# A mixed attention and Fourier kernel on one core: mirrored sequence rows regrouped by period, copied back by one DMA per batch, with a new instruction order

## The chip, the core and the metric

The kernel runs on one NeuronCore of one Trainium2 chip. The time is the device time of one execution, in microseconds (us). The core has five engines with an instruction queue of their own each: TensorE (PE, matrix products and transposes), VectorE (DVE), ScalarE (ACT), GpSimd (POOL) and SyncE (SP). In this kernel SP does nothing but issue DMAs, one after the other, and nearly every DMA of the kernel goes through it. Sixteen DMA engines move the bytes.

## What is computed

```python
# attention, for each batch and head:  q, k, v: (8, 8, 576, 64), omega: (128, 64)
def phi(x):                              # x is q or k times 64**-0.25
    h = einsum('bhsd,md->bhsm', x, omega) - sum(x * x, -1, keepdims=True) / 2
    return exp(h - max(h, -1, keepdims=True)) / sqrt(128)
kv  = einsum('bhsm,bhsd->bhmd', phi(k), v);  z = sum(phi(k), axis=2)
att = einsum('bhsm,bhmd->bhsd', phi(q), kv) / (einsum('bhsm,bhm->bhs', phi(q), z) + 1e-6)
x   = att, heads side by side            # (8, 576, 512)
# Fourier mixing and a two-layer block
u   = x + real(fft(fft(x, axis=1), axis=2))
un  = (u - mean(u)) / sqrt(var(u) + 1e-6)          # over the last axis
out = u + relu(un @ w_ch1) @ w_ch2                 # 512 -> 2048 -> 512
```

## The kernel before

**Two stages.** The first stage (0 to 446 us of the profile) does the attention and the Fourier mixing of all 8 batches, converts the weights, which arrive as 64-bit numbers, to 32 bits (`narrow`), prepares sums of weight blocks for the second stage (`w2_parts`), and already runs the two-layer block for the first four tiles of 128 rows (`plain`, L1017 and L1040). The second stage (446 us to the end) runs the two-layer block for the other 4,096 rows in 8 blocks of 512, with products arranged as in Strassen's scheme (L1224 and L1403).

**Attention.** A unit of work is a pair of heads; there are 4 per batch, 32 in all, and three streams of them run side by side. One pair loads k and q (L376, L379) and v (L384), transposes them on PE (L505, moved out of PSUM by ACT in L516), multiplies with omega (L587), takes maxima on DVE (L531) and exponentials on ACT (L548), forms the sums over the keys (L621), transposes phi(q) (L505 again, moved out by ACT in L522), multiplies (L669, L677) and divides (L686 to L698). A partition of the loaded tiles holds 9 consecutive rows of the sequence (R = 9).

**Rows and slots.** The result of a batch is kept in a tile x of 128 partitions and 5 slots of 512 numbers. The rows stand in an order that suits a real Fourier transform over the sequence: slot 0 holds rows t, slot 3 rows 288 + t, slots 1 and 2 the mirrored rows 288 - t and 576 - t, and slot 4 what is left. Before the change, the rows t of a slot are grouped by the half of an 18-row period that they lie in (`half`, 64 partitions each), then by remainder (`QUAD`), then by period (16). This order is made in `evicted` (L522): a 128x256 eviction writes 16 consecutive numbers at a time, and the third group is read backwards as a whole (`back`).

**Mixing.** `mix` folds x, multiplies with tables of cosines and sines (`_tables`, L781 to L840), and `residual` adds the result to x slot by slot (L879, L880, on POOL or DVE) and stores the sums to a DRAM buffer `us` in natural row order. Slots 0, 3 and 4 go there directly, each in two DMAs (L894). For slots 0 and 3 the destination of such a DMA is four remainders by 16 periods, the remainders outermost. Slots 1 and 2 hold mirrored rows, whose order has to be reversed; each is stored to a second DRAM buffer `uh` by one DMA (L886), and when all five slots have landed, 8 DMAs (L911) copy `uh` to `us`, two for each of four remainders, reading the periods backwards. Each moves 64 KB, written as 4 outer pieces by 32 rows of 128 numbers.

**Who reads it.** `norm_of` loads a tile of 128 rows of `us` (L920 into u), takes the statistics on DVE (L947 to L949), a power on POOL (L951), scales on DVE (L953) and transposes on PE (L957). In the first stage 8 such tiles are made: four for `plain`, four for the first block of the second stage. The four final sums of `plain` load the same rows again (L920 into ur).

**What sets the order.** Each engine runs a fixed list of instructions. The lists are written by `Listing.run`: every stream of work yields steps with an engine, a planned duration and planned events, and the string `PICKS` says for each turn which waiting stream goes next. The planned durations and events decide only the order; the real waits are semaphores that follow from which instruction reads what another one wrote. So an instruction that is listed too early holds up all that stands behind it on its engine, and a DMA on SP whose data isn't ready holds up all later DMAs. The second stage is listed without `PICKS`, by the planner's own rule.

Of the kernel before, what the change touches and what calls it, by code (L numbers as in the profile page):

```python
# [17 lines left out]
F32 = mybir.dt.float32  # L18
# [10 lines left out]
QUAD = (2, 4, 6, 8)  # L29
MIRROR = (7, 5, 3, 1)  # L30
ORDER_R = (0,) + QUAD + MIRROR
# [8 lines left out]
class Clock(NamedTuple):  # L40
# [23 lines left out]
    "130dc0debe3dedefedeef3aae8bfg0cijbkfa98j88i8i8if2gfQehgjeeeekfjk7fklhggdgeidhiQfed7gfgbga8898jiiaigf"  # L64
    "ig9IHaaebbibbgilhhfhfgbjkhhhliOJKTfe9ich888i88jh9hg8aijkfhPg8hhdhhfdidfdfg8799ggI8i8jaghgl88ekkfejff"
    "fdjhdjgfjdegghk1IccjejeiidLcibkihek798kjml6jMgec9c9Gg6iiiShefjjJg7jejj66bgkakddkejmeediigihfbhfifhde"
    "fjifkkbaOkkcllmfi8ijNakeeemkhcM7oo7ckk6obM9nmfj9bad97hfmf8lfmmd8nnkHUdeeediicS7ifedbfifgcfefggeegcai"
    "dgejciegdgcgfciehffQihffhhdhdhhda79li07hi64678j9jii577gdjji5gdghachcfcgdOif5gcFgfbfbcfge5i6697k7l37a"
    "9gidbehdjc6hhkd7lc8jbejkl9bhihjja6cfi76jcjcbf8lmfnDciidbhg5icVfghkoba9aagadgfekbdbh9KG9k7ggdlie7cjai"
    "bmgegigfalkijfIcegdjeTejdgfQehd88i864NcbfagH8g7ghkdfdd6hfeijbgbff67eahacf6g8g7be54N6e9ccdafbdecccb5d"  # L70
    "hccd957hh5he86l878gg77ldWddifdfhejgg6gRi6Gdafjb8aQdkdj5cgddfigfdafhdQficdhefe9hhhfL55f5hai6b696inlhh"
    "h6MecljcnijVlcdcchhhcf96afdijiif5bjQhfhgghHIeiabjiijg87jjcf6d5iijiiMaajha87mWekfkjUjgjbeifddg5gihf5N"
    "4ehbceh4bfibcgabcckefcfdjjfhedcklfiighed4ifkfdlemcbdd655kjme9dmb5hiVkckkal79jjlEdmijhkhnnklod5hhgmfF"
    "mcmdeedllkeedjId787hLF8ahahhg68fkgjifggkh5iedhijkeddeglhf7ckk3ejbkmk7ck8f7ik6jj5j5744mn76nnjjeiaakj5"
    "4mfgogjiU5Ofll6ecjgfflTkjg5Ob8hceflafi5675lk869llan9VV3775ll86kf7khjaQi6gkklic5lhk5nnndfgikk59aiicja"
    "ifjbfhihaebdmngffbI61efcgdh0cgf89EO6ii9hceOcbafdfda8d27995fc5bPa779dgdeIR9QSa8Md9cg9d99eb3bag79JMbbc"
    "ceddbe9PKbbaacccc32d9de8e5379dfKb9f2ded6adbc79cd8ceca8e9dceHaHeebbaaeabc98K5977b8aee8hifdbcdfccad9d3"
    "added6Ocae85d233babb9c9c8c463c83K97a777cbdc687daIb9df9cabgae9769egeHb993ee89P5e8biafiihbec6jk8hkkFgj"
    "153ki32fdgL3a484f5e4bcb4b97bL62eeFefcffKI2d7d794abIJ4134a79917GK3ab46b9962738a7cc79cc33aLMJI64effbcc"
    "b4ebdfObec2ccLceacec68aOa8ee625G69c9M6bddcJd7a98aa27bbLb5dc6eag5b6f5fee98bd91dfddBfgQdfQI5477523c881"  # L80
    "a0b3444Ebb9a089aKa88aba8a177bcdeHLOa13ad76cc4Fd8c7cca80a64966667d547840965bc8bbe65507dcb1d732D697174"
    "6968G5624408A7E66A35555555011001110"
# [167 lines left out]
def _tables(S, DM):  # L250

    half, rr, ph = (a.ravel() for a in np.meshgrid(np.arange(2), QUAD, np.arange(16), indexing="ij"))
    t = 9 * (2 * ph + half) + rr
    t0 = 9 * (2 * np.arange(32)[None, :] + np.arange(2)[:, None])
    ks = [np.concatenate([t[64 * g : 64 * g + 64], S // 2 - t[64 * g : 64 * g + 64], t0[g]]) for g in range(2)]
    turns = [(t[:, None] * k) % S for k in ks]
    turns.append((np.tile(t0.ravel(), 2)[:, None] * np.concatenate(ks)) % S)
    turn = np.concatenate(turns, axis=1)  # L260
    ang = 2.0 * np.pi * turn / S
    cs = np.cos(ang)
    sn = np.where(turn * 2 % S == 0, 0.0, np.sin(ang))

    d = np.arange(DM // 4)[:, None]
    k = np.arange(DM // 2 + 1)
    k = np.concatenate([k[k % 4 == 0], k[k % 4 == 2], k[k % 2 == 1]])[None, :]  # L270
    turn = (d * k) % DM
    cd = np.cos(2.0 * np.pi * turn / DM)
    turn = (np.where((d == 0) & (k % 2 == 1), DM // 4, d) * k) % DM
    sd = np.where(turn * 2 % DM == 0, 0.0, np.sin(2.0 * np.pi * turn / DM))
    return {
        n: np.ascontiguousarray(a).astype(np.float32)
        for n, a in dict(cs=cs, sn=sn, cd=cd, sd=sd).items()
    }
# [3 lines left out]
def kernel(  # L282
# [86 lines left out]
    def loads():  # L369
        for n in range(B * NP):  # L370
            b, pr = divmod(n, NP)
            h = slice(2 * pr, 2 * pr + 2)
            rows = "i (p r) d -> (i p) r d"
            yield Step(SP, 0.45, 3.0, take=("kq",), kb=288)
            kq = ld.tile([P, 2 * R, D], F32, name="kq", tag="kq")
            nc.sync.dma_start(kq[:, 0:R, :], k[b, h].rearrange(rows, r=R))  # L376
            kqs[n] = kq
            yield Step(SP, 0.45, 3.6, makes=("kq", n), kb=288, bias=-2.98)
            nc.sync.dma_start(kq[:, R : 2 * R, :], q[b, h].rearrange(rows, r=R))  # L379

    def load_v(n):
        b, pr = divmod(n, NP)
        yield Step(SP, 0.6, 4.0, take=(f"vd{n % NV}",), makes=("vd", n), kb=500, bias=0.52)
        nc.sync.dma_start(  # L384
            vds[n % NV][:, :, 0:D],
            v[b, 2 * pr : 2 * pr + 2].rearrange("i (p r) d -> (i p) r d", r=R),
        )
# [27 lines left out]
    def load_tables():  # L415
        yield Step(NONE, after=(("kq", 2),))
        for n, a in tabs.items():
            yield Step(SP, 1.0, 4.0, makes=n, kb=a.nbytes / 1024, bias=0.92)
            src = nc.inline_tensor(a, name="k_" + n).ap()
            for p0, p1 in ((0, 96), (96, a.shape[0])):  # L420
                nc.sync.dma_start(tab_sb[n][p0:p1], src[p0:p1])
# [35 lines left out]
    def weights():  # L457
# [4 lines left out]
        for i, (dst, src) in enumerate(parts):  # L462
# [3 lines left out]
            else:  # L466
                yield Step(SP, 0.5, 4.2, take=("slab",), makes=("raw", i), kb=512)
# [9 lines left out]
    uh = [dram.tile([8, 2, 16, DM], F32, name=f"uh{b}") for b in range(B)]  # L477
# [10 lines left out]
    def transposed(src, name, groups, after, makes, give, back=None, order=None):  # L488
# [3 lines left out]
        for j0, j1 in groups:  # L492
# [13 lines left out]
            yield Fork(evicted(dst, b, j0, j1, makes, (j0, j1) == back, order))  # L506
        return dst

    def evicted(dst, b, j0, j1, makes, back, order):
# [3 lines left out]
        ps = ps[:, :, ::-1] if back else ps  # L513
# [5 lines left out]
        dst = dst.rearrange("q c p -> q (c p)").rearrange("q (h s c t) -> q s c h t", h=h, s=s, t=t)  # L519
        ps = ps.rearrange("q c (h t s) -> q s c h t", h=h, s=s)  # L520
        for i in range(s):
            nc.scalar.activation(out=dst[:, i], in_=ps[:, i], func=AF.Copy)  # L522
# [32 lines left out]
    def attn(n):  # L555
# [74 lines left out]
        def keep():  # L630
# [19 lines left out]
            (5, R),  # L650
# [13 lines left out]
        for i in range(2):  # L664
            for c in range(4):
                j0, back = (5, 1) if c in (1, 2) else (1, 0)
                c0 = 128 * (j0 + 2 * (i ^ back) + c % 2)
                for g in range(2):
                    nc.tensor.matmul(  # L669
                        ndp[D * g : D * g + D, i, (D + 1) * c : (D + 1) * (c + 1)],  # L670
                        lhsT=flat[:, c0 + D * g : c0 + D * g + D],
                        rhs=kvs[0][:, i, :],
                    )
# [36 lines left out]
    def mix(b):  # L710
# [102 lines left out]
        for c in range(NC3):  # L813
# [39 lines left out]
            yield Fork(residual(b, c, x, abb))  # L853

    def residual(b, c, x, abb):
# [18 lines left out]
        def summed(g, left, right):  # L874
# [9 lines left out]
            yield Step(SP, 0.42 if slot in (1, 2) else 0.84, 2.6, makes=("us", b, slot), kb=2 * np_, bias=-0.92)  # L884
            if slot in (1, 2):
                nc.sync.dma_start(uh[b][:, 2 - slot], u)  # L886
                return
            for s in range(2):
                rows = rows_of(b, s)
                if slot == 4:  # L890
                    rows = rows[0]
                else:
                    rows = rows[2::2, 16 * (slot == 3) : 16 * (slot == 3) + 16]
# [5 lines left out]
        yield Step(NONE, after=(("us", b, c if c < NL else 4),), give=("bmp",), bias=1.09)  # L899
        if c == NL:  # L900
            yield Step(
                SP, 3.4, 4.0,
                after=tuple(("us", b, i) for i in range(5)),
                makes=("us", b),
                give=(f"x{b % 2}",),
                kb=512,
            )
            for s in range(2):
                for n, r in enumerate(MIRROR):
                    back = uh[b][4 * (1 - s) + n].rearrange("e t (i d) -> (e t) i d", i=4)  # L910
                    nc.sync.dma_start(  # L911
                        rows_of(b, s)[r].rearrange("p (i d) -> i p d", i=4),
                        back[::-1].rearrange("p i d -> i p d"),
                    )

    def rows_of(b, s):
        return us[S * b : S * (b + 1), :].rearrange("(p s r) d -> s r p d", s=2, r=R)[s]
# [20 lines left out]
    def norm_of(j, t, i, pool, dst):  # L938

        yield Step(SP, 0.5, 3.0, take=("u",), kb=256)  # L940
# [107 lines left out]
    def rest(t, b, yp):  # L1048
        yield Step(SP, 0.5, 2.7, take=("ur",), kb=256)
# [41 lines left out]
    def w2_parts():  # L1091
# [22 lines left out]
        for i, made_of in (  # L1114
# [16 lines left out]
            yield Step(SP, 2.2, 4.5, after=(("w2t", i),), kb=7 * 256, makes=("w2l", i))  # L1131
# [409 lines left out]
```

## Time and profile before

| what | value |
|---|---|
| median of 3 runs | 1207.48 us (1206.46 to 1210.01) |
| the profiled execution: its own time, its span in the profile | 1205.58 us, 1203.7 us |
| granted TensorE clock, mean | 0.993 |
| PE busy in the first stage (446 us) and the second (757.7 us) | 419.2 us, 752.3 us |
| DVE busy in the two stages | 321.6 us, 381.7 us |
| ACT busy in the two stages | 297.2 us, 170.1 us |
| POOL busy in the two stages | 180.3 us, 238.7 us |
| DMAs L911 (uh to us): count, median SP time of one issue | 64, 628 ns |
| DMAs L894 (x to us): the same | 48, 538 ns |
| DMAs L886 (x to uh): the same | 16, 599 ns |

The profile is of one execution, so durations read from it are summed against its own 1205.58 us; the 1.9 us between that and the span lie around the profiled instructions. The median of the runs is 1.9 us above the profiled execution. A row of the table of stretches gives the stretch in us from the start and its length, then the busy time of each engine with the number of instructions begun, then the granted PE clock as a share of full speed, the mean busy share of the 16 DMA engines, and GB/s. A row of a timeline gives start, length, engine, line, operation, tiles written and read, the number of merged instructions, and in square brackets how long the engine had been idle before and what it waited for. "L911" is line 911 of the kernel.

### The profile page before, as it was taken

Reading aid. Unit: us, or ns where it says so; the run is one execution under the profiler, and the core shown is the slowest. Engines: PE = TensorE matmul, PEld = TensorE weight load, DVE = VectorE, ACT = ScalarE, POOL = GpSimd, SP = SyncE. Lnnn points to the kernel's source line nnn. Section 1 sums busy time; section 2 is a strip of 40 time slices with the busy share of each in tenths; the row PEclk is TensorE's granted clock in tenths of the full one; section 3 lists DMA queues with packets and bytes.
Section 4 is the critical chain, followed back from the end, with each engine's and each line's share of the span. In section 5 each row is a group of like instructions: output and inputs, shape, how many; then the busy total and the mean of one; then the engine's idle time right before and its main releaser. Section 6 shows DMA issues by size and latency. Waiting matters only on the chain.

```text
span 1203.7 us, 31915 instructions
## 1 busy us (share of the span) xinstructions
PE 1171.5 (97%) x12753; PEld 1049.2 (87%) x12753; DVE 703.3 (58%) x1496; ACT 467.3 (39%) x1585; POOL 419.0 (35%) x490
## 2 busy tenths in 40 slices
PE   7898999999999999999999999999999999999998
PEld 6777888779959778998998999999899899899898
DVE  4896998977664553572472474374275276267245
ACT  6887888767646112222222222222222222222211
POOL 2453443542433324314323323422421431430421
PEclk9998999999989999999999999999999999999999
DMA  9655756657553343482383294195086176167145
GB/s 261 184 144 161 219 178 193 187 156 228 187 166 111 115 133 117 161 283 91 122 293 120 82 295 158 43 303 190 9 297 194 44 257 207 62 224 249 62 162 189
DMA packets 148452, 205.71 MB, mean 171 GB/s; under 512 B 48720, under 2 KB 62288, under 8 KB 148304
## 3 DMA queue, kind: packets, MB, share of 16 engines
q1 hardware_dynamic: 147936, 203.54, 53.6%
q8 instruction: 101, 1.65, 0.6%
q14 instruction: 47, 0.39, 0.1%
q10 hardware_dynamic: 368, 0.13, 0.0%
HBM read 171.90 MB, written 35.91 MB: 173 GB/s over the span
## 4 chain that ended last, share of the span: by engine, by line
PE 78%; DMA 1%; DVE 1%; SPq 1%; ACT 0%; issue 0%; DVEq 0%; ACTq 0%
PE banks L1224 32%; PE banks L1403 29%; PE banks L1017 4%; PE banks L1040 3%; PE banks L505 2%; PE banks L587 2%; PE banks L957 1%; PE banks L669 1%; PE banks L621 1%; PE banks L829 1%; PE banks L781 1%; DMA u<-us 1%; DMA kq<-in_q_dram 1%; PE banks L791 1%; PE banks L840 0%; ACT e L548 0%
## 5 line engine op out<-in xcount | busy, mean ns | idle before, releaser
L1210 DVE CUSTOM_DVE_ANT_0 hid<-banks,s 128x256 f32<-128x256 f32 x192 | 79.7, 423 | 255.3 <-PE banks L1224 250.4
L1403 PE MATMUL banks<-wl,sums 128*128 128x128 f32 x1792 | 217.5, 275 | 0.0
L1403 PEld LDWEIGHTS banks<-wl,sums 128*128 128x128 f32 x1792 | 208.9, 192 | 0.5
L1238 ACT ACTIVATE s<-banks 128x256 f32<-128x256 f32 x192 | 73.7, 384 | 260.6 <-PE banks L1224 245.8
L548 ACT ACTIVATE e<-banks,nmx 128x128 f32<-128x128 f32 x576 | 163.2, 422 | 29.1 <-DVE nmx L531 26.2
L1224 PE MATMUL banks<-unT,w 128*128 128x256 f32 x704 | 167.5, 379 | 0.0
L1224 PEld LDWEIGHTS banks<-unT,w 128*128 128x128 f32 x704 | 132.7, 190 | 17.9 <-issue 0.5
L1378 ACT ACTIVATE s<-banks 128x128 f32<-128x128 f32 x168 | 46.6, 278 | 242.5 <-PE banks L1403 195.9
L1224 PE MATMUL banks<-tt,w1s 128*128 128x256 f32 x512 | 126.2, 379 | 0.0
L1291 POOL TENSOR_TENSOR hs<-hid 128x256 f32<-128x256 f32 x64 | 46.5, 726 | 205.0 <-DVE hid L1210 178.6
L1224 PEld LDWEIGHTS banks<-tt,w1s 128*128 128x128 f32 x512 | 97.2, 190 | 13.3
L531 DVE TENSOR_REDUCE nmx<-banks 128x8 f32<-128x1024 f32 (+1 forms) x96 | 89.4, 951 | 23.0 <-PE banks L587 21.7
L1383 DVE TENSOR_TENSOR part<-banks,s 128x128 f32<-128x128 f32 x168 | 48.9, 291 | 89.2 <-PE banks L1403 89.0
L1403 PE MATMUL banks<-wl,hid 128*128 128x128 f32 x768 | 97.6, 275 | 0.0
L1403 PEld LDWEIGHTS banks<-wl,hid 128*128 128x128 f32 x768 | 93.5, 192 | 1.2
L1291 POOL TENSOR_TENSOR hs<-hid,hs 128x256 f32<-128x256 f32 x64 | 46.5, 728 | 120.1 <-issue 95.2
L587 PE MATMUL banks<-om,kqT 64*64 64x128 f32 x2304 | 79.4, 277 | 2.0 <-issue 0.7
L1224 PE MATMUL banks<-unT,w1s 128*128 128x256 f32 x320 | 80.6, 379 | 0.0
L587 PEld LDWEIGHTS banks<-om,kqT 64*64 64x64 f32 x2304 | 64.3, 134 | 14.0 <-issue 6.0
L951 POOL TENSOR_TENSOR rstd<-rstd,mhalf 128x1 f32<-128x1 f32 x36 | 24.5, 682 | 146.4 <-DVE rstd L949 146.4
L1403 PE MATMUL banks<-wl,hs 128*128 128x128 f32 x576 | 74.9, 275 | 0.4 <-DVE part L1383 0.4
L1403 PEld LDWEIGHTS banks<-wl,hs 128*128 128x128 f32 x576 | 70.0, 192 | 0.9 <-DVE part L1383 0.6
(126 smaller groups left out, 1958.1 us busy)
## 6 DMA issues: line engine op xcount, KB each, us to landing
wl<-w2l SPq DMA_DIRECT2D x392, 256.0 KB
raw<-in_moe_w_ch_dram SPq DMA_DIRECT2D x32, 512.0 KB
kq<-in_k_dram SPq DMA_DIRECT2D x32, 288.0 KB
kq<-in_q_dram SPq DMA_DIRECT2D x32, 288.0 KB
vd<-in_v_dram SPq DMA_DIRECT2D x32, 288.0 KB
u<-us SPq DMA_DIRECT2D x36, 256.0 KB
ur<-us SPq DMA_DIRECT2D x36, 256.0 KB
out_dram<-ur SPq DMA_DIRECT2D x34, 256.0 KB
```

The source lines that it names most:

```text
L531: nc.vector.tensor_reduce(nmx[:, :, 0:num], pps[:, :, 0 : MF * num].rearrange("p b (c m) -> p b c m", m=MF), axis=AX.X, op=ALU.max, negate ...
L548: nc.scalar.activation(out=e[:, c + (i if num == 1 else 0), :], in_=pps[:, i, MF * c : MF * c + MF], func=AF.Exp, bias=nmx[:, i, c : c + 1],)
L587: nc.tensor.matmul(pps[cols, c, MF * m : MF * m + MF], lhsT=kqT[rows, j, cols], rhs=om2[rows, :],)
L1017: nc.tensor.matmul(hp[:, 0:TP], lhsT=w1[:, dc, 128 * fc : 128 * fc + 128], rhs=unTs[key][:, dc, :], start=(dc == 0), stop=(dc == NDC - 1),)
L1040: nc.tensor.matmul(yp[:, 0:DM], lhsT=hs[fc][:, 128 * i : 128 * i + 128], rhs=w2[:, fc, :], start=(fc == 0), stop=(fc == NFC - 1),)
L1210: nc.vector._custom_dve(TENSOR_ADD_SAT, out=o, in0=ps, in1=sb, s0=FMAX, s1=0.0)
L1224: nc.tensor.matmul(ps[:, 0:HT], lhsT=left(dc), rhs=right(dc), start=start and dc == 0, stop=(dc == D2 - 1), skip_group_check=True,)
L1238: nc.scalar.activation(out=s[:], in_=ps[:, 0:HT], func=AF.Copy)
L1291: nc.gpsimd.tensor_tensor(out=o, in0=l, in1=r, op=op)
L1378: nc.scalar.activation(out=s[:], in_=ps[:, 0:128], func=AF.Copy)
L1383: nc.vector.tensor_tensor(out=part[:, t, 128 * m : 128 * m + 128], in0=ps[:, 0:128], in1=saved[with_][:], op=ALU.add,)
L1403: nc.tensor.matmul(ps[:, 0:128], lhsT=left[:, f], rhs=wls[j, i, n][:, f], start=start and f == 0, stop=(f == 3), skip_group_check=True,)
```

## The change

The rows of a slot are now grouped by even and odd remainder (`EVEN` and `ODD`, 64 partitions each), then by period, then by remainder. Four consequences follow in the code:

- In `evicted` the number of ACT instructions stays, but the 128x256 ones now write with the four remainders innermost, so that consecutive numbers in reading order land 4 numbers (16 bytes) apart, and the second of each two reads both the remainders and the periods backwards.
- `mirrored` takes the place of the two L886 stores. It stands behind both sums and sends slots 1 and 2 together in two DMAs of 256 KB.
- One DMA of 512 KB takes the place of the 8 DMAs L911. It copies 8 consecutive rows for each of 32 periods, the periods read backwards, in 16 outer pieces by 32 rows of 256 numbers.
- The stores of slots 0 and 3 (two DMAs each, as before) now have 16 periods outermost and four remainders inside.

The planned durations of several DMAs are changed, and `PICKS` is a new string (1,851 picks; before, 1,835). The tables keep their shapes. In the core of the diff, `PICKS`, the changed offsets of the L669 products and seven changed planned durations are left out:

```diff
-QUAD = (2, 4, 6, 8)
-MIRROR = (7, 5, 3, 1)
-ORDER_R = (0,) + QUAD + MIRROR
+EVEN = (8, 6, 4, 2)
+ODD = (7, 5, 3, 1)
+ORDER_R = (0,) + EVEN + ODD
...
-    half, rr, ph = (a.ravel() for a in np.meshgrid(np.arange(2), QUAD, np.arange(16), indexing="ij"))
-    t = 9 * (2 * ph + half) + rr
+    t = np.array([18 * ph + r for rows in (EVEN, ODD) for ph in range(16) for r in rows])
...
-    uh = [dram.tile([8, 2, 16, DM], F32, name=f"uh{b}") for b in range(B)]
+    uh = [dram.tile([32, 8, DM], F32, name=f"uh{b}") for b in range(B)]
...
-        ps = ps[:, :, ::-1] if back else ps
...
-        dst = dst.rearrange("q c p -> q (c p)").rearrange("q (h s c t) -> q s c h t", h=h, s=s, t=t)
+        dst = dst.rearrange("q c p -> q (c p)").rearrange("q (h s t c) -> q s c h t", h=h, s=s, t=t)
         ps = ps.rearrange("q c (h t s) -> q s c h t", h=h, s=s)
         for i in range(s):
-            nc.scalar.activation(out=dst[:, i], in_=ps[:, i], func=AF.Copy)
+            of = ps[:, i, ::-1, :, ::-1] if i and j0 else ps[:, i]
+            nc.scalar.activation(out=dst[:, i], in_=of, func=AF.Copy)
...
+        yield Fork(mirrored(b, x))
+
+    def mirrored(b, x):
+        yield Step(SP, 1.15, 2.6, after=(("sum", b, 1), ("sum", b, 2)), makes=("uh", b), kb=512, bias=-0.92)
+        for s in range(2):
+            nc.sync.dma_start(
+                uh[b].rearrange("(e t) (n s) d -> s (t n) e d", e=2, s=2)[s],
+                x[64 * s : 64 * s + 64, 2:0:-1, :],
+            )
...
             if slot in (1, 2):
-                nc.sync.dma_start(uh[b][:, 2 - slot], u)
+                yield Step(NONE, makes=("sum", b, slot))
                 return
+            yield Step(SP, 1.15, 2.6, makes=("us", b, slot), kb=2 * np_, bias=-0.92)
+            p0 = 16 * (slot == 3)
             for s in range(2):
-                rows = rows_of(b, s)
                 if slot == 4:
-                    rows = rows[0]
+                    rows = rows_of(b)[:, 9 * s, :]
                 else:
-                    rows = rows[2::2, 16 * (slot == 3) : 16 * (slot == 3) + 16]
+                    rows = rows_of(b)[p0 : p0 + 16, (8, 7)[s] :: -2, :][:, 0:4, :]
                 nc.sync.dma_start(rows, u[np_ // 2 * s : np_ // 2 * (s + 1)])
...
+            yield Step(SP, 0.7, 3.0, after=(("uh", b),), makes=("back", b), kb=512)
+            ahead = rows_of(b)[:, 10:18, :].rearrange("p r d -> p (r d)")
+            back = uh[b][::-1].rearrange("p r d -> p (r d)")
+            nc.sync.dma_start(
+                *(a.rearrange("p (i d) -> i p d", i=16) for a in (ahead, back))
+            )
...
-            for s in range(2):
-                for n, r in enumerate(MIRROR):
-                    back = uh[b][4 * (1 - s) + n].rearrange("e t (i d) -> (e t) i d", i=4)
-                    nc.sync.dma_start(
-                        rows_of(b, s)[r].rearrange("p (i d) -> i p d", i=4),
-                        back[::-1].rearrange("p i d -> i p d"),
-                    )
```

## Prediction

> **What bounds the kernel now.** I began with the table of stretches, cut where the behaviour changes (columns: stretch, length, then busy time of PE, PE weight loads, DVE, ACT and POOL, granted clock, DMA share, GB/s):
>
> ```profile
> 0.00:102.00 102.00, 88.03 (x2099) 74.20 (x2100) 78.30 (x150) 83.31 (x305) 41.40 (x43) 1.00 0.70 195
> 102.00:120.00 18.00, 14.05 (x215) 12.78 (x215) 10.19 (x28) 10.93 (x37) 5.64 (x6) 0.81 0.51 145
> 120.00:328.00 208.00, 201.41 (x4263) 174.57 (x4258) 173.16 (x369) 161.79 (x587) 92.44 (x86) 1.00 0.65 195
> 328.00:360.00 32.00, 29.74 (x273) 17.80 (x272) 20.64 (x40) 12.36 (x46) 11.49 (x11) 0.89 0.51 156
> 360.00:446.00 86.00, 86.00 (x881) 66.93 (x878) 39.32 (x108) 28.78 (x105) 29.34 (x36) 1.00 0.37 111
> ```
>
> The second stage (446 us to the end, PE busy 752.3 of 757.7) has none of the changed steps; I leave it as it is. In the first, PE is busy 419.2 of 446 us. Of its 26.8 us of idleness 4.9 lie before its first instruction. Two short stretches stand out, 102-120 and 328-360: PE idles 3.95 and 2.26 us there, and only there the granted clock falls. I call them A and B. The rest, 15.6 us, is scattered in small pieces. In 120-328 PE (97%), DVE (83%) and ACT (78%) are all well loaded, so work taken off one of them alone is worth little there; what is worth something is a stall of all three.
>
> What ends A and B stands in the waits and in the timelines of DVE and PE:
>
> ```profile
> DVE st L947 <- DMA u<-us: 10.1, 2, 5.7
> ```
>
> ```profile
> 107.07 0.69 DVE L947 BATCH_NORM_STATS2 st<-u 128x6 f32<-128x512 f32 x1 [4.36 <-DMA u<-us]
> ...
> 344.00 0.69 DVE L947 BATCH_NORM_STATS2 st<-u 128x6 f32<-128x512 f32 x1 [5.74 <-DMA u<-us]
> ```
>
> ```profile
> 110.16 1.12 PE L957 MATMUL banks<-ident,u 128*128 128x128 f32 x4 [3.95 <-DVE u L953]
> ...
> 350.79 0.81 PE L781 MATMUL banks<-cs_sb,fold 128*128 128x160 f32 x4 [2.04 <-ACT e L548]
> ```
>
> Twice DVE stands before the statistics of a tile whose rows have not come back from DRAM; maxima (L531) stand behind them, exponentials wait for the maxima, PE for those. So the order lists L947 earlier than the load can deliver. Why it is late shows on SP's timeline:
>
> ```profile
> 90.43 8.03 SPq L911 DMA_DIRECT2D us<-uh  x8
> 98.56 0.62 SPq L384 DMA_DIRECT2D vd<-in_v_dram  x1
> ...
> 102.33 0.33 SPq L920 DMA_DIRECT2D u<-us  x1
> ```
>
> and in the DMA share while the mirrored rows travel:
>
> ```profile
> 94.00:96.00 2.00, 2.00 (x40) 1.72 (x32) 2.00 (x5) 1.94 (x8) 1.15 (x1) 1.00 0.28 99
> 96.00:98.00 2.00, 2.00 (x39) 1.30 (x37) 1.99 (x4) 2.00 (x9) 1.21 (x1) 1.00 0.29 87
> 98.00:100.00 2.00, 2.00 (x89) 1.56 (x92) 2.00 (x4) 1.86 (x10) 1.58 (x2) 1.00 0.33 95
> ...
> 106.00:108.00 2.00, 0.21 (x5) 0.12 (x4) 0.88 (x2) 0.00 (x0) 0.00 (x0) 1.00 0.92 275
> ```
>
> The eight copies hold SP for 8 us, and what is queued behind them (v, weights, then the load of u) starts 8 us late. While they run, the DMA engines are busy to 0.28-0.33, about a quarter. The packet records between 94.73 and 101.98 us count 1,024 packets of 512 B at 27 ns each: 27.6 us of engine time, which takes 7.25 us, so on about 4 engines. Then the delayed loads come at once and the share is 0.92 until u is there.
>
> **The change, part by part.**
>
> *Copies.* Out go 64 issues of L911, 51.5 us of SP summed over the eight batches of the timeline. In come 8 issues. A DMA with far more pieces (v, L384, 1,152 of 256 B) takes SP 0.55-0.62 us, so pieces don't set the issue time; 8 x 0.65 = 5 us. SP saves some 46 us, about 5.8 a batch. The transfer becomes 512 packets of 1 KB; the nearest row, the 1,028 B packets of the tables, has 50 ns, so 25.6 us of engine time, as before. On 16 engines that is 1.6 us, on 4 it is 6.4. No row shows this form; the Trainium skill ("DMA: Bandwidth & Descriptors", "Why a DMA increments its semaphore by 16 and not by 1") has the engines be the largest number up to 16 that divides the slowest dimension of both sides. That gives 4 before, as the share says, and 16 after. I take 1.6.
>
> *Stores.* Still six issues a batch at 0.54 us. Slots 0 and 3 are 256 packets of 2 KB a batch (0.11 us each over the first stage): 28 us of engine time, by the same rule on 4 engines, 7.0 us, after it 1.8. The mirrored stores stay two issues of 0.6 us a batch; 8 engines become 16, 3.5 us to 1.8. Together the four busiest engines lose 5.3 + 5.2 + 1.7 = 12 us a batch, 98 us of the stage. Loads of k, q, v and weights use these engines too and land when their slowest share does.
>
> *Waits.* `mirrored` waits for both sums of slots 1 and 2, and the copy for its landing. Behind them on SP are loads of later pairs. Before, SP waited for each sum singly (up to 12.4 us for a POOL sum) and L911 for the landing of uh 2.2 us at most, so a wait is moved rather than added: price -2 to +2.2 us a batch on SP, taken as 0, since the loads behind it run a pair ahead. If that cover is gone, kq waits come up on PE (L505 on kq: 2.9 us in all now).
>
> *Evictions (L522).* 192 ACT instructions, as before, 128 of them writing with a step of 16 B.
>
> ```profile
> L516 ACT ACTIVATE kqT<-banks 128x512 f32<-128x512 f32 x64 | 38.7, 639 | 14.7 <-PE banks L505 14.5
> L522 ACT ACTIVATE qeT<-banks 128x256 f32<-128x256 f32 x128 | 42.3, 430 | 8.7 <-PE banks L505 8.6
> ...
> L867 DVE SCALAR_TENSOR_TENSOR bmp<-banks,bmp 128x64 f32<-128x64 f32 x32 | 10.5, 327 | 0.0
> ```
>
> The Trainium skill speaks against this part: "SBUF — State Buffer", "Door 1: The DMA port swizzle", says that every access crossing to a new 16-byte line pays a penalty. If that were one more element time (0.85 ns, from L516: 639 ns for 512 elements, 311 for 128), it adds 0.22 us x 128 = 28 us of ACT. L867 writes with just this step, on DVE: 327 ns for 64 elements, where the other DVE rows (510 elements 687, 384 elements 552, so 1.07 ns each, and 702 for 512 in the same operation) make about 223; the 104 ns left also hold a PSUM read and a scalar operand, so 0 to 1.6 ns per element. The step of 8 B in L870 costs 3 ns in 281. A gain is excluded: writing 16 in a row already runs at L516's slope. I take 0, as with L870; the range keeps 28 us of ACT.
>
> *PE.* Same products, other offsets: 0.
>
> *Order.* `PICKS` is new and no row shows what it is worth. Below: all scattered idleness, -15.6 us. Above: new stalls as large as A and B. I take +3 us, half of B, because another fixed order has early listings of its own.
>
> **The sum.** A: PE gets back 3.95 us of idleness, and the clock: it was at 0.50 for 6.83 us (109.3-116.1), 3.4 us of work. DVE's stall of 4.36 us goes: with the copies out in 0.65 us and landed some 2-3 us after the queue clears at 95.75, u is asked for at about 97.5 instead of 102.3. A is worth 7.35. B: 2.26 us of idleness and again 6.83 us at half clock (351.6-358.4). Here the Trainium skill ("TensorE: Matmul & The Clock Gate", "Part 1: The HAM clock gate") wants an idle window of some 3.4 us before the clock falls; the trace has it fall after gaps of 2.04 and 0.22 us. By the rule B is worth 2.26, by the row 5.7; I follow the row. But B's load stands behind stores (L894) that remain, so half: 2.8. Total -7.35 - 2.8 + 3 = -7.2: 1205.58 - 7.2 = 1198.4 for a profiled execution, and 1.9 more for the median: 1200.3. From 360 us on PE has no gap, so what is saved earlier arrives there undiminished. Next late after A and B: DVE and ACT in 120-328.
>
> **Rivals.** About 0.3% (3.6 us) is what a measurement here can tell from no change.
>
> *Taken back.* The waits on data are only the last of several; with SP and the DMA engines freed, DVE (173 of 208 us) and ACT set the pace and the new order has stalls of A's size. For it: three engines near full. Against: at A all three stood still. Median 1205-1209, say 1207. The same if the copy doesn't spread over 16 engines.
>
> *More.* Loads land earlier everywhere, POOL and ACT wait less for weights (28 us now), and half of the scattered idleness goes too: 1200.3 - 7.8 = 1192.5.
>
> *Slower: the evictions.* With a full extra element time ACT gets 28 us, most of it before 328 us, where it is busy 256 of 328 us. If half lies on the path, 14 - 7 = +7: 1214.5. It decides from about 0.43 ns per element, where half of it eats the 7 us.
>
> **Chances.** Likeliest 0.52 (1196.5 to 1203.9); more 0.18; taken back 0.20; slower 0.10. So faster 0.70, same 0.20, slower 0.10. Eight in ten: 1191 to 1208.5, which cuts the slower case, the best of the larger gain and the edge of the third.
>
> **What would show it.** L911 with 8 issues near 0.65 us; no stretch of 6 us at a DMA share of 0.3; L947 waiting under 4 us for u in all; fewer than two half-clock stretches in the first stage; L522 still near 430 ns; the first stage near 439 us, the second 757-758. I am wrong if L522 grows by over 0.1 us, or if the copies are short and the stage is not.

## The result, and the profile after

The changed kernel takes 1199.99 us, the median of 6 runs (1196.51 to 1201.42), against 1206.97 us before (6 runs on the same chip). The ratio is 0.9938, with a 95% interval of 0.9915 to 0.9961: 0.62% faster. The profiled execution took 1200.75 us with a span of 1198.9 us. In the profile the second stage starts at 441.08 us instead of 445.99 and is as long as before (757.8 us), so the first stage is 4.9 us shorter in these two executions.

The table of stretches of the kernel after, cut at the same times as before (columns as in the prediction):

```profile
0.00:102.00 102.00, 87.67 (x2089) 73.02 (x2089) 77.81 (x146) 87.85 (x300) 43.62 (x44) 1.00 0.71 203
102.00:120.00 18.00, 16.72 (x296) 14.84 (x295) 16.36 (x43) 15.58 (x48) 10.77 (x11) 1.00 0.41 123
120.00:328.00 208.00, 201.73 (x4182) 173.58 (x4182) 164.40 (x338) 173.09 (x591) 95.98 (x95) 0.99 0.61 184
328.00:360.00 32.00, 32.00 (x345) 21.93 (x337) 17.88 (x39) 16.09 (x52) 21.43 (x21) 1.00 0.65 214
```

Both stalls are gone. In 102-120 us (A) PE is busy 16.7 us instead of 14.05 and the clock stays at 1.00; in 328-360 us (B) PE has no idle time, at full clock. DVE's wait for the load of u is 2.9 us in all instead of 10.1:

```profile
DVE st L951 <- DMA u<-us: 2.9, 2, 1.7
```

SP's timeline around the first load of u, and the rows of the DMA issues (count, size, median time to landing):

```profile
97.22 0.59 SPq L912 DMA_DIRECT2D us<-uh  x1
...
102.72 0.33 SPq L924 DMA_DIRECT2D u<-us  x1
```

```profile
us<-uh SPq DMA_DIRECT2D x8, 512.0 KB, 5.4
```

The one copy (now L912) costs SP 0.59 us where the eight cost 8.03, and lands in 5.4 us (median). The packet records show the 512 packets of 1 KB of this one leaving within 3.2 us; the forecast had 1.6. The load of u is not asked for earlier than before (102.72 us against 102.33), because the new order issues the copy later (97.22 us against 90.43). What became shorter is the time from the copy to the load, 5.5 us instead of 11.9. DVE's wait there falls from 4.36 to 1.20 us because the statistics can start 2.8 us after the load is issued instead of 4.7, and because DVE comes to them later: it begins to wait at 104.3 us, before at 102.7.

One thing goes the other way. ACT is busy 319.7 us in the first 446 us instead of 297.2, and the groups of ACT in the first stage name the cause, the evictions (L522 before, now L521):

```profile
L521 ACT ACTIVATE qeT<-banks 128x256 f32<-128x256 f32 x128 | 70.2, 738 | 7.0 <-PE banks L504 6.8
L514 ACT ACTIVATE kqT<-banks 128x512 f32<-128x512 f32 x64 | 39.8, 655 | 17.0 <-PE banks L504 15.2 <-issue 1.3 <-ACT qeT L521 0.4
```

The same 128 evictions took 42.3 us, 430 ns each; now it is 70.2 us and 738 ns. A 128x256 eviction lasts longer than a 128x512 one. Evictions overlap (128 times 738 ns is more than the 70.2 us), so the price is read from the busy time: it grew by 27.9 us, or 0.218 us per instruction and 0.85 ns per number, one full element time more.

So the total is close to the forecast, but it is made of other parts. The experiments take them apart.

### The profile page after: what moved, and what is told of

Read it like the earlier page. It is cut to its first block, busy times and chain, and to the rows that moved or that the text cites. A ratio compares the mean times of both kernels' runs of the same rounds, so it can differ in the third digit from the quotient of the medians.

```text
span 1198.9 us, 31843 instructions
## 1 busy us (share of the span) xinstructions
PE 1171.2 (98%) x12753; PEld 1048.6 (87%) x12753; DVE 702.7 (59%) x1479; ACT 488.6 (41%) x1583; POOL 438.0 (37%) x509
## 4 chain that ended last, share of the span: by engine, by line
PE 67%; DVE 0%; issue 0%; ACT 0%; DVEq 0%
PE banks L1228 32%; PE banks L1407 29%; PE banks L1044 2%; PE banks L961 1%; PE banks L1021 1%; PE banks L827 0%; PE banks L779 0%; PE banks L667 0%; PE banks L789 0%; PE banks L838 0%; DVE u L957 0%; DVE part L1387 0%; PE banks L675 0%; ACT qeT L521 0%; DVE ur L1339 0%
## 5 line engine op out<-in xcount | busy, mean ns | idle before, releaser
L521 ACT ACTIVATE qeT<-banks 128x256 f32<-128x256 f32 (+1 forms) x192 | 79.2, 593 | 10.7 <-PE banks L504 10.5
L586 PEld LDWEIGHTS banks<-om,kqT 64*64 64x64 f32 x2304 | 64.5, 134 | 14.3 <-ACT kqT L514 4.1
```

The lines of the kernel that those rows point to most:

```text
L521: nc.scalar.activation(out=dst[:, i], in_=of, func=AF.Copy)
L586: nc.tensor.matmul(pps[cols, c, MF * m : MF * m + MF], lhsT=kqT[rows, j, cols], rhs=om2[rows, :],)
```

## The experiments

Each kernel ran beside the kernel before on the same chip, and "ratio" is to that, with its 95% interval. The rows come from four sets of runs, whose medians of the kernel before lie between 1206.88 and 1207.41 us, so a difference of half a us between two rows can come from the set alone.

| kernel | median us | ratio | first stage ends, us |
|---|---|---|---|
| after | 1199.99 | 0.9938 (0.9915 to 0.9961) | 441.08 |
| old order, new layout and DMAs | 1198.05 | 0.9920 (0.9901 to 0.9940) | 441.60 |
| new order, old layout and DMAs | 1206.65 | 0.9996 (0.9987 to 1.0006) | 446.20 |
| after, 8 copies of 4 pieces | 1209.21 | 1.0021 (1.0004 to 1.0037) | 451.11 |
| after, one copy of 4 pieces | 1206.15 | 0.9987 (0.9976 to 0.9997) | 446.81 |
| after, 8 copies of 16 pieces | 1204.56 | 0.9983 (0.9974 to 0.9993) | 448.14 |
| after, first attempt at stores of 4 pieces | 1198.69 | 0.9931 (0.9917 to 0.9946) | 438.35 |
| after, stores of 4 pieces (rows of two slots in another order) | 1203.82 | 0.9963 (0.9946 to 0.9980) | 446.26 |
| after, evictions that write in a row | 1191.94 | 0.9876 (0.9851 to 0.9900) | 430.71 |
| evictions in a row, old order | 1192.33 | 0.9874 (0.9855 to 0.9893) | 435.96 |
| evictions in a row, 8 copies of 4 pieces | 1200.55 | 0.9939 (0.9923 to 0.9955) | 441.32 |
| evictions in a row, stores of 4 pieces (rows of two slots in another order) | 1197.01 | 0.9918 (0.9898 to 0.9939) | 435.78 |

My theory was that the copies and the spread over the DMA engines removed A and B. The rival was that the new order did it, by listing the statistics where the data is there.

**The new operations in the old order.** The edit to the kernel before: the whole diff without `PICKS` and without the new steps. The two mirrored stores are issued at whichever of the two sums is listed second.

```diff
             if slot in (1, 2):
-                nc.sync.dma_start(uh[b][:, 2 - slot], u)
+                summed_slots.setdefault(b, set()).add(slot)
+                if len(summed_slots[b]) == 2:
+                    for s in range(2):
+                        nc.sync.dma_start(..., x[64 * s : 64 * s + 64, 2:0:-1, :])
                 return
```

> The order of before (its 1,835 picks and planned durations), with everything else of the change: rows regrouped, evictions with a 16-byte step, the mirrored rows stored by two DMAs behind both sums, one copy of 512 KB in 16 outer pieces, stores in 16 outer pieces. Theory (the copies and the spread over the DMA engines removed the two stalls on the load of u): stall A goes by itself, DVE waits under 1 us for u there, and in spite of the slower evictions the time is 1200 to 1203 us, at least half of the gain. Rival (the new order removed them, by listing the statistics later): A and B stay, the evictions add, and the time is 1207 to 1213 us.

Measured: 1198.05 us, below the range that I gave the theory. DVE has no wait for u left that the profile lists, and both stretches are free of the stalls (PE busy 17.72 of 18 us and 32.00 of 32):

```profile
102.00:120.00 18.00, 17.72 (x330) 15.85 (x328) 15.67 (x46) 16.00 (x47) 8.63 (x10) 1.00 0.48 129
...
328.00:360.00 32.00, 32.00 (x394) 21.82 (x384) 22.61 (x43) 15.93 (x54) 11.92 (x11) 1.00 0.51 165
```

Here the copy is issued at 91.54 us and u is asked for at 98.48, close to the 97.5 of the forecast.

**The old operations in the new order.** The reverse edit to the kernel after. Of it are shown the mirrored stores and the copies; the layout, the evictions and the other stores go back as well:

```diff
-        for s in range(2):
-            nc.sync.dma_start(uh[b].rearrange(...)[s], x[64 * s : 64 * s + 64, 2:0:-1, :])
+        for slot in (1, 2):
+            nc.sync.dma_start(uh[b][:, 2 - slot], x[:, slot, :])
...
-            nc.sync.dma_start(*(a.rearrange("p (i d) -> i p d", i=16) for a in (ahead, back)))
+            for s in range(2):
+                for n, r in enumerate(MIRROR):
+                    ...
```

> The new order (1,851 picks and the new planned durations), with the old layout: old evictions, each mirrored slot stored by one DMA of 8 outer pieces (both issued where the new order has the mirrored store), 8 copies of 64 KB at the place of the one, stores in 4 outer pieces. Theory (copies and spread): the stall on u comes back, 1206 to 1212 us. Rival (order): 1195 to 1200 us, as after or better, since the evictions are the fast ones.

Measured: 1206.65 us, ratio 0.9996. Its stretch, DVE's wait for u and SP's timeline show stall A again:

```profile
102.00:120.00 18.00, 11.34 (x179) 10.63 (x173) 10.59 (x22) 8.61 (x33) 7.45 (x8) 0.72 0.48 143
```

```profile
DVE st L952 <- DMA u<-us: 13.8, 4, 7.0
```

```profile
93.50 8.48 SPq L912 DMA_DIRECT2D us<-uh  x8
...
105.81 0.33 SPq L925 DMA_DIRECT2D u<-us  x1
```

The copies hold SP for 8.48 us, u is asked for at 105.8 us, and PE is busy 11.3 of 18 us at a mean clock of 0.72. But stall B is not there:

```profile
328.00:360.00 32.00, 32.00 (x447) 22.40 (x446) 21.36 (x44) 13.47 (x47) 23.45 (x24) 1.00 0.51 157
```

DVE still waits for u there, 1.36 us instead of 5.74, and PE doesn't idle. So the two stalls have different answers. For A the rival is out: with the old operations A stays in either order. B goes with the new operations or with the new order, and either is enough, so for B the rival holds as well as the theory. In this kernel the loss of B is outweighed: A is deeper than before (PE idle 6.66 us instead of 3.95, half clock for 10.24 us instead of 6.83), and the clock falls once more at 147.5 us, for 6.83 us. In all, the new order with the old operations and the fast evictions is worth between -0.13% and +0.06%.

**The copy in its old form.** The kernel after, with

```diff
-            ahead = rows_of(b)[:, 10:18, :].rearrange("p r d -> p (r d)")
-            back = uh[b][::-1].rearrange("p r d -> p (r d)")
-            nc.sync.dma_start(*(a.rearrange("p (i d) -> i p d", i=16) for a in (ahead, back)))
+            for n in range(8):
+                ahead = rows_of(b)[:, 10 + n, :]
+                back = uh[b][::-1][:, n, :]
+                nc.sync.dma_start(*(a.rearrange("p (i d) -> i p d", i=4) for a in (ahead, back)))
```

> The changed kernel and its order, with the one copy of 512 KB split again into 8 of 64 KB, each in 4 outer pieces by 32 rows of 128 numbers as before the change. SP time per batch goes from 0.6 to 5-8 us and the copy back to a quarter of the DMA engines. Theory: at A the load of u is asked for about 5 us later, DVE waits 5 to 6 us for it instead of 1.2, the clock falls again, and the time is 1205 to 1209 us. Rival: the new order leaves room for it, 1200 to 1202 us.

Measured: 1209.21 us, 9.2 more than after, just above the range, and slower than before. Two stretches while the copies run show the quarter share again:

```profile
101.00:103.00 2.00, 1.85 (x92) 1.61 (x84) 1.64 (x3) 2.00 (x10) 0.82 (x2) 1.00 0.26 71
103.00:105.00 2.00, 2.00 (x27) 1.78 (x19) 1.90 (x6) 2.00 (x11) 0.00 (x0) 1.00 0.27 75
```

Stall A is back, with the fall of the clock. Its stretch, what DVE waits for u, and what PE waits for that:

```profile
102.00:120.00 18.00, 12.51 (x175) 11.02 (x171) 11.30 (x27) 10.60 (x36) 5.66 (x7) 0.82 0.48 133
```

```profile
DVE st L952 <- DMA u<-us: 7.4, 2, 5.7
```

```profile
PE banks L962 <- DVE u L958: 5.3, 1, 5.3
```

B does not come back (PE busy 32.00 of 32 us in 328-360), as the new order alone keeps it away.

**SP's time or the spread?** First one copy on a quarter of the engines (`i=4` in the new form):

> The changed kernel with its one copy in 4 outer pieces by 32 rows of 1,024 numbers instead of 16 by 256. SP still issues one DMA of 0.6 us, but the 512 KB go over 4 engines: 128 packets of 4 KB at some 0.16-0.2 us are 5 to 6.4 us on each of them. If it is SP's time that mattered (8 copies cost 9 us), this stays within 2 us of 1200. If it is the spread over the engines, it lies near the 1209 us of the 8 copies.

Measured: 1206.15 us, 6.2 more than after, between the two forecasts. Then eight copies on all engines:

```diff
+            for n in range(8):
+                ahead = rows_of(b)[4 * n : 4 * n + 4, 10:18, :].rearrange("p r d -> p (r d)")
+                back = uh[b][::-1][4 * n : 4 * n + 4].rearrange("p r d -> p (r d)")
+                nc.sync.dma_start(*(a.rearrange("p (i d) -> i p d", i=16) for a in (ahead, back)))
```

> The changed kernel with its one copy cut into 8 DMAs of 64 KB, for four periods each, all in 16 outer pieces of 1 KB rows: SP is held for 8 issues again, but all engines share the bytes. If SP's time mattered, 1206 to 1210 us; if the spread did, 1200 to 1203.

Measured: 1204.56 us, 4.6 more than after, again between the two ranges. Each alone brings half of the loss or more: the intervals of both lie above that of after and below that of the two together. So the loss belongs to SP's time and to the spread together. The load of u has to wait until the copy has been issued and has landed, and each half alone makes it late. From the first issue of the copy to the load of u pass 5.5 us in after, 9.3 with one copy on 4 engines and 10.0 with eight on 4. With eight on 16 it is 6.5 us, and the load then lands later. DVE's longest wait for u is 4.9 us with one copy on 4 engines and 4.6 us with eight on 16. Which of the two halves costs more is not settled, as their intervals overlap.

**The stores.** A first attempt cut the 16 periods into four groups of four, outermost:

```diff
+                if slot != 4:
+                    rows = rows.rearrange("(a p) r d -> a p r d", a=4)
```

> The changed kernel with the stores of slots 0 and 3 in 4 outer pieces (the 16 periods cut into four groups of four, outermost), the same bytes and the same number of DMAs. Theory: 256 packets of 2 KB a batch go back to 4 engines, 7 us on each instead of 1.8; loads behind them land later, and the time rises by 1 to 4 us. If the stores don't matter, it stays within 1 us of 1200.

Measured: 1198.69 us. It says nothing on the stores. The shape in the instruction records is the one of after, 16 outer by 4: the two dimensions had been merged again. It is a repeat of the kernel after, and agrees with it within the intervals. The second attempt puts the remainders outermost, which the instruction records show as 4 outer by 16:

```diff
+                if slot != 4:
+                    rows = rows_of(b)[p0 : p0 + 16, (2, 1)[s] :: 2, :][:, 0:4, :].rearrange("p r d -> r p d")
```

> The changed kernel with the stores of slots 0 and 3 truly in 4 outer pieces: remainders outermost, 16 periods inside, as before the change (the earlier attempt was merged back into 16 pieces). Same bytes, same number of DMAs; the rows of these two slots reach the right batch and remainder class but in another order, so this part of the computation is changed. Theory: 7 us a batch on each of 4 engines instead of 1.8, loads behind them late, 1201 to 1204 us. If the stores don't matter, 1197.5 to 1200.5.

Measured: 1203.82 us, 3.8 more than after and 5.1 more than its repeat. The intervals of this run and of after overlap in part, those of this run and the repeat only touch. What the stores delay is again the load of u at A, where PE is busy 14.0 of 18 us at a mean clock of 0.81. DVE's waits for u, and the stop of PE:

```profile
DVE st L953 <- DMA u<-us: 8.3, 4, 4.3
```

```profile
111.29 1.11 PE L963 MATMUL banks<-ident,u 128*128 128x128 f32 x4 [3.98 <-DVE u L959]
```

At B PE doesn't idle in this run either.

**The evictions.** The same transposition with the loops of the access pattern the other way round: the four remainders are walked innermost, so the write is 64 numbers in a row, and the step falls on the read from PSUM.

```diff
-        dst = dst.rearrange("q c p -> q (c p)").rearrange("q (h s t c) -> q s c h t", h=h, s=s, t=t)
-        ps = ps.rearrange("q c (h t s) -> q s c h t", h=h, s=s)
+        dst = dst.rearrange("q c p -> q (c p)").rearrange("q (h s t c) -> q s h t c", h=h, s=s, t=t)
+        ps = ps.rearrange("q c (h t s) -> q s h t c", h=h, s=s)
         for i in range(s):
-            of = ps[:, i, ::-1, :, ::-1] if i and j0 else ps[:, i]
+            of = ps[:, i, :, ::-1, ::-1] if i and j0 else ps[:, i]
```

> The changed kernel with one edit: the 128x256 evictions walk the four remainders innermost, so that they write 64 numbers in a row and read PSUM with a step of 512 B instead. Same values, same places. If the write step of 16 B is what lengthened them (738 ns mean against 430 before, 28 us of ACT in all) and a read step is free, the mean returns to about 430 ns, ACT's busy time in the first stage falls from 320 to about 292 us, and the time to 1195-1198 us if the evictions lie on the path, or stays within 1 us of 1200 if ACT has room. If the read step costs as much, both stay.

Measured: 1191.94 us, 8.1 less than after and 1.2% below before. It beats both kernels, and lies below either range. The group of evictions, and its stretches:

```profile
L521 ACT ACTIVATE qeT<-banks 128x256 f32<-128x256 f32 x128 | 42.4, 436 | 8.1 <-PE banks L504 7.7
```

```profile
102.00:120.00 18.00, 18.00 (x307) 16.49 (x307) 17.55 (x44) 13.23 (x42) 10.77 (x12) 1.00 0.53 150
120.00:328.00 208.00, 202.09 (x4134) 171.84 (x4127) 168.33 (x352) 160.46 (x590) 100.71 (x99) 1.00 0.62 188
```

The read step of 512 B in PSUM costs nothing that can be seen against the evictions of before, which read PSUM with a step of 8 B (436 ns against 430). ACT is back to 160 of 208 us in the long stretch, and no fall of the clock is recorded in the first stage.

**Do the parts add?** Three more runs stand on the version with the fast evictions. Its operations in the old order:

> The order of before with the new layout and DMAs, and the evictions that write 64 numbers in a row. Theory (the new order is worth about nothing, the evictions cost 8 us under it): 1189 to 1194 us, and evictions near 435 ns. If the old order hid the slow evictions better than the new one, 1196 to 1199 us.

Measured: 1192.33 us. A second time the order makes no difference. In the old order the fast evictions bring 5.7 us (1198.05 to 1192.33, intervals apart), in the new one 8.1. Then the copy in its old form:

> The version with the evictions that write in a row (1191.9 us), with the copy in the old form again: 8 DMAs of 64 KB in 4 outer pieces. If copy form and evictions cost independently, 9 us more: 1199 to 1203. If the slow evictions are what left no room for a late load, so that the copies cost less here: 1194 to 1197.

Measured: 1200.55 us, 8.6 more; under the slow evictions it was 9.2. And the stores in 4 pieces:

> The same stores in 4 outer pieces, on the version with the evictions that write in a row (1191.9 us). The rows of slots 0 and 3 are again in another order. Theory: 2 to 5 us more, 1194 to 1197. If the stores don't matter, 1191 to 1193.

Measured: 1197.01 us, 5.1 more, at the upper end of the range. Here the two intervals overlap at their edges (0.9851 to 0.9900 and 0.9898 to 0.9939), so the stores' cost is shown by two runs that agree rather than by one that is clear. The evictions add to the order, to the copies and to the stores within the noise: writing in a row brings 5.7, 8.1, 8.7 and 6.8 us in the four pairs. Whether copies and stores add to each other was not tried; both act on the same load of u at A.

## Why the prediction was right, and where it was not

The time was right (1200.3 forecast, 1199.99 measured), the working only in part, and that the number fits so well is luck. Three terms of the sum missed. In the new order the DMAs are worth 14.7 us where the sum had 10.2, the order is worth nothing where it had +3, and the evictions cost 8.1 us where it had 0. The first two make the forecast about 7.5 us too slow, the third 8 us too fast. The prediction's own sign of being wrong, L522 longer by over 0.1 us, came true: it grew by 0.31 us.

- **A** was forecast to go, and went in whichever order. It comes back with the old operations (PE idle 6.7 us), with the old copies alone (5.3 us) and with the old form of the stores alone (4.0 us). The mechanism, copies that delay the load of u, is shown by the pair of order runs and by the runs on the copy. That u would be asked for at about 97.5 us held in the old order (98.48); in the new one it is asked for at 102.72, and DVE's wait is short because u lands sooner after that and DVE comes later.
- **B** was credited by half, because its load stands behind stores that remain. That was wrong: it is gone in full, with the new operations in the old order and with the old operations in the new order. Which of the new DMAs removes it in the old order was not tried, since the runs on copies and stores all have the new order, in which B doesn't come back.
- **Stores**: I counted that the four busiest engines lose 12 us a batch, and then gave the stores no share in the sum. They are worth 4 to 5 us, the copies 9, and for both the runs show the loss at A.
- **Together** the new DMAs are worth 15.1 us in the old order with the fast evictions (1207.41 to 1192.33 us), and 14.7 in the new one (1206.65 to 1191.94). The forecast had 7.35 + 2.8 = 10.2. Copies (8.6 to 9.2) and stores (3.8 to 5.1) would make up 12.4 to 14.3 of it, if they add; what the mirrored stores bring was not measured by itself.
- **Evictions** were taken at 0 and cost 8.1 us here, 5.7 to 8.7 over the four pairs. This step failed. I laid the value on L870, an 8-byte step on DVE, though L867 with the very step of 16 B left room up to 1.6 ns. The rule of the Trainium skill that I set aside ("SBUF — State Buffer", "Door 1: The DMA port swizzle") was right in kind for ACT, and the price that I had worked out from it as one more element time is what the trace shows, 0.85 ns per number and 27.9 us in all. Of these 27.9 us a fifth to a third lies on the path. My case "slower" assumed half, against 7 us for all the rest; at the share measured, DMAs worth 15 us more than pay for it. PE's listed waits for these evictions rise only from 0.7 us to 3.2 us. That the rest acts through the queue of ACT, by what stands behind them, is argued and was not measured alone.
- **Order** was put at +3 us and is worth 0 within the noise: ratio 0.9996 with the old operations, 1192.33 us (old) against 1191.94 (new) with the new operations and evictions that write in a row, 1198.05 against 1199.99 with those that write with a step. With the old operations this 0 is a sum, B gone and A deeper.
- **Waits of `mirrored`**, taken at 0: no run tried them alone, so their price stays open. What SP's list shows of waits for sums at the mirrored stores fell: for POOL's sums it is 29.2 us before (L886), 15.1 with the new operations in the old order, and 5.6 after (L857).
- **SP's time**: 46.1 us of L911 become 5.1 us, 41 saved where I had 46; the 51.5 us were read from merged rows of the timeline, gaps included.
- **The clock**: I followed the trace's row against the page named in the prediction, and took back 3.4 us of work at each stall. Both falls are gone with the stalls. In the kernel after one short fall is left in the first stage (3.4 us at half clock from 143.1 us, after a gap of 2.51 us). So a gap under 3 us can cost clock here, but need not: a gap of 2.77 us in the version with fast evictions, and one of 2.20 in the repeat of after, had no fall behind them.

## What to carry to other kernels

Read how many DMA engines a transfer uses from the share they show while little else runs: 0.26 for a copy of 512 KB means that three quarters of them stand idle, and here the load that had to wait for this copy came late. When a layout is changed for DMAs, look at what the engine that writes the layout now does per element; here the access pattern could be walked the other way round, so that the step fell on the side where it was free. And a total that fits doesn't prove the terms: here runs that swapped the order and the operations, and took the evictions alone, showed what the time alone could not.

## What the runs showed that was not expected

Writing 32-bit numbers to SBUF with a step of 16 B cost ACT one element time more each (0.85 ns), while reading PSUM with a step of 512 B cost nothing more than the step of 8 B before (436 against 430 ns for a 128x256 eviction).

PE stopped in the middle of a group of products, with nothing that the profile shows to wait for: 2.51 us in after, 2.77 with the fast evictions, 2.58 with eight copies of 4 pieces (all at L620), 2.18 with the new operations in the old order (at L668). "Issue" in the row stands for time in which the engine waited for nothing that the profile shows.

```profile
142.92 0.96 PE L620 MATMUL banks<-vd,e 64*64 64x65 f32 x26 [2.51 <-issue]
```

In the two stretches around it in the kernel after the DMA share is 1.01 and 1.17:

```profile
140.00:142.00 2.00, 0.41 (x28) 0.28 (x18) 1.81 (x3) 2.00 (x10) 0.02 (x1) 1.00 1.01 366
142.00:144.00 2.00, 1.08 (x27) 0.96 (x28) 0.01 (x1) 0.97 (x3) 1.93 (x2) 0.79 1.17 330
```

Late loading of PE's own instructions would fit, since instructions come by DMA too (queues q8 and q14 in the profile's list of queues), and the records speak for it. The line differs between the two orders, but the place counted in PE's instructions does not: in all twelve changed kernels the stop lies before the 5,826th or 5,827th record of products and weight loads, and before the change there is a gap of 0.68 us at the same place. In each of the twelve a packet of 16 KB of q8 is under way (in after from 140.55 us, for 1.04 us), and PE goes on 1.3 to 1.6 us after its end. The packet itself is not slow: the median of q8's packets in the first stage takes 1.00 us. So if it comes late, it starts late; whether PE is too fast for it there or the busy DMA engines hold its start up is open. No run moved it, and the cause is not shown. In the kernel after the stop costs 2.51 us and, behind it, 3.4 us at half clock.
